# A new order of loads and work for attention and a feed-forward pair on one core

## The chip, the cores and the metric

The kernel runs on one core of a Trainium2 chip. The metric is device time in microseconds of one execution. The core has five engines with their own instruction queues: TensorE (PE, matmuls), VectorE (DVE), ScalarE (ACT), GpSimd (POOL) and SyncE (SP). Each runs its queue in order and waits at semaphores for the others. DMAs are issued by SP and by POOL.

## The reference

Four sequences of 768 positions and 8 heads of 64 are attended with a window, and the result goes through a feed-forward pair without a nonlinearity but relu and square:

```python
scores = scale * np.matmul(q, k.transpose(0, 1, 3, 2))      # q, k, v: (4, 8, 768, 64)
keep = is_global | is_local       # key < 8, or 0 <= query - key < 96
bias = -slopes[:, None, None] * dist[None, :, :]
a = softmax(np.where(keep, scores + bias, -1e9))
x = np.matmul(a, v).transpose(0, 2, 1, 3).reshape(3072, 512)
r = np.maximum(x @ w_in, 0.0)     # w_in: (512, 2048)
out = (r * r) @ w_out             # w_out: (2048, 512)
```

Inputs and output are float32; the kernel computes in bfloat16 with float32 sums.

## The kernel before

**Tiles.** The 3072 rows are cut into 24 tiles of 128 (0 to 23), six to a sequence; two tiles make one of 12 blocks. Tiles 0, 6, 12 and 18 are the first of their sequences. Because the window is shorter than a tile, a tile needs the keys and values of itself and of the tile before, whose first 8 columns are overwritten with the global keys (`gk`) and first 8 rows with the global values (`gv`).

**Attention of a tile j.** `ld` or `load` brings q, k and v, cast to bfloat16, through POOL's DMA queue (tile 0's q and k come over SP in float32). Up to tile 7 PE transposes q and k (`tr.0.j`, `tr.1.j`, L506) and ACT or DVE copies them out (`T.0.j`, `T.1.j`, L429/L433); from tile 8 on an SP DMA transposes them (`T.j`, L537). `sc.j.0` (L599) makes the scores: 16 matmuls into four banks, 8 into two for a first tile; `bias` (L579) precedes for tiles 0 to 2. `exp.j` (ACT, L665) empties a bank each. From tile 3 on `mul.j` (DVE, L690) multiplies with the masks `E`, or `E0` for a first tile, which `E0.0` and `E0.1` make (L439, L440). `pv` (L748) multiplies with v, `norm` (L778, L779) divides, and `trx` with `xT` (PE and a copy; from tile 8 on an SP DMA) transposes the result. `gate.j` (L480) is a tiny DVE write that lets POOL's load of tile j go.

**Feed-forward.** Blocks 0 and 1 take the first weight in the plain form: `s1.b.s` (L1061), `relu` (L865/L867), `sq` (L1098/L1100). All others, and the second weight from block 1 on, use seven products in place of eight: sums and differences of x (`xs`), of the weights (`isum`, `wsum`) and of hidden values (`sum`), then products `h.b.g.p1` to `p7` (L950) and `s2.b.p1` to `p7` (L1212). Between h products, ACT or DVE copies a bank out (`u`, L429/L433), DVE adds and applies relu (`c`, L995) and ACT or DVE squares (`q`, L1015/L1017). Block 0's second stage is plain (L1339). `part` and `o` (L1287) take the results out, `st` stores them. `wsum` and `isum` need all of a half's weights (`ld.win.s`, `ld.wout.s`).

**Order.** No scheduler runs on the chip or in the build: the text `ORDER` is a list of some 1,220 words, written out, and `Plan.run` emits each named operation at its place. `exp.3.0.1` is a name, `@A`, `@V`, `@P` choose ACT, DVE or POOL, and digits behind a colon are the PSUM banks, of which there are eight. Each engine's queue is its words of this list in order; nothing else fixes when an operation runs but what it waits for. POOL's loads run ahead of their place in the list as far as their buffers are free; `gv.j@P` copies stand in the same POOL queue. SP's queue holds `T.j`, `xT.j` and `st`.

At the start eight matmuls on zeros run (L372), and the list's `warm` adds eight more behind `tr.0.0` (L529 to L534). `COPY` names five tiles (14, 15, 19, 20, 22) whose keys are copied whole into `kl` (L703 to L719), so that the next tile's scores needn't wait for `gk`, which may only overwrite keys once the own tile's scores are made. `JOIN` could name stretches of scores that are made together with the preceding one (L615 to L630); it is empty. Four float32 buffers `u` are used in turn (L897). In the last block the product p3 is made in two parts of 192 and 64 columns, and each part's output operation waits for its own (L1261).

Of the kernel before, what the change touches and what calls it, by code (L numbers as in the profile page):

```python
# [63 lines left out]
tr.0.4:7 ld.q.5 ld.v.4 norm.2.1 mul.3.1 relu.0.6@A s1.0.3#2 gv.2@P pv.3.0:3 norm.3.0 trx.2:5 T.0.4@A pv.3.1:6
ld.win.1.0 norm.3.1 ld.win.0.1 xT.2@A sc.4.0:1047 exp.4.1.1 exp.4.1.0 tr.1.5:3 T.1.5@A s1.0.2:5 trx.3:6 xT.3@V
ld.win.0.0 ld.win.5.0 s1.0.2#2 s1.0.2#3 s1.0.2#4 relu.0.3@V exp.4.0.1 ld.v.5 gv.3@P exp.4.0.0 gk.4@V sq.0.6@V
relu.0.2@A s1.1.3:7 ld.win.7.0 relu.1.3@A load.6 s1.1.6:0 mul.4.1 tr.0.5:6 mul.4.0 sq.0.3@V s1.1.2:3 T.0.5@A ld.wout.3
pv.4.0:2 ld.wout.1 sq.0.2@V sc.5.0:4157 ld.wout.0 s1.0.4:6 relu.1.2@A exp.5.1.1 s1.0.1:3 sq.1.3@A exp.5.0.0 relu.0.4@V
s1.1.4:7 ld.wout.2 norm.4.0 pv.4.1:4 gv.4@P norm.4.1 sq.0.4@A load.7 exp.5.1.0 sq.1.2@A relu.1.4@A s1.0.0:6 gate.9
ld.wout.4 mul.5.0 s1.0.0#2 sq.1.4@A s1.0.0#3 s1.1.5:2 trx.4:1 exp.5.0.1 relu.1.6@V s1.1.1:4 ld.wout.5 s1.0.1#2  # L70
relu.1.1@A E0.1 mul.5.1 relu.1.5@A pv.5.0:7 s1.1.7:0 s1.1.0:5 sq.1.1@V norm.5.0 ld.wout.6 E0.0 sq.1.5@V tr.1.6:4
sq.1.6@A pv.5.1:2 relu.1.7@A tr.0.6:7 s1.0.0#4 norm.5.1 xT.4@A sq.1.7@A h.2.0.p2:0 ld.wout.7 T.1.6@V h.2.1.p2:1
trx.5:2 xT.5@V relu.1.0@A sq.1.0@A gate.14 h.2.0.p1:5 xs.2.0 s1.0.5:4 sum.1.2 s1.0.7:2 relu.0.1@A xs.2.1 gate.10
sum.1.0 sum.1.1 relu.0.0@A T.0.6@A sc.6.0:36 wsum.0.0 sum.1.3 sq.0.0@A sq.0.1@A s2.0.0.0:7 relu.0.7@A s2.0.1.0 load.9
exp.6.0.0 xs.2.2 s2.0.2.0 exp.6.1.0 s2.0.3.0 s2.0.0.1:2 s2.0.1.1 wsum.2.0 relu.0.5@A sq.0.7@A s2.0.2.1 load.8 mul.6.0
wsum.1.0 s2.0.3.1 tr.0.7:3 tr.1.7:6 gate.15 isum.0.0 h.2.1.p1:4 T.0.7@A s2.0.4.0 isum.0.1 s2.1.p1.0:3 isum.3.1 T.1.7@A
sq.0.5@A pv.6.0:6 isum.1.1 s2.0.4.1 s2.0.5.1 u.2.0.1@A c.2.0.c11 s2.0.5.0 gate.11 u.2.1.1@A h.2.1.p6 q.2.0.c11@A
isum.1.0 T.8 s2.0.6.1 u.2.1.2@A s2.0.6.0 isum.3.0 pv.6.1:0 h.2.0.p6 wsum.2.1 wsum.0.1 s2.1.p1.1 s2.0.7.1 c.2.1.c11
norm.6.0 gate.13 o.0.1@V st.0.1 s2.0.7.0 h.2.1.p7 part.1.p1@A s2.1.p6.0 u.2.0.2@A o.0.0@A u.2.1.3@A h.2.0.p7 h.2.1.p4
T.9 norm.6.1 wsum.3.0 u.2.0.3@A sc.7.0:1762 c.2.1.c21@A wsum.1.1 h.2.1.p5:0 c.2.1.c22 q.2.1.c11@A s2.1.p2.0:4  # L80
exp.7.1.0 exp.7.0.0 isum.2.1 load.10 h.2.0.p4 exp.7.0.1 mul.7.0 exp.7.1.1 s2.1.p2.1 isum.2.0 s2.2.p1.0:7 q.2.1.c21@A
mul.7.1 h.2.0.p5:1 s2.1.p6.1 part.1.p6@A trx.6:6 gate.12 c.2.0.c21@A load.12 pv.7.0:2 xT.6@A c.2.0.c22 q.2.1.c22@A
q.2.0.c22@A s2.2.p1.1 h.2.1.p3 s2.1.p7.0 wsum.3.1 o.1.p2 norm.7.0 h.2.0.p3 pv.7.1:5 s2.1.p7.1 q.2.0.c21@A st.0.0
c.2.1.c12 s2.1.p5.0 s2.1.p5.1 part.1.p7@A q.2.1.c12@A s2.1.p4.0 T.10 s2.1.p4.1 c.2.0.c12 gk.7@V q.2.0.c12@A o.1.p5
o.1.p4@A sc.8.0:6201 st.1.1 part.2.p1@A s2.1.p3.0 norm.7.1 sum.2.0 sum.2.1 s2.1.p3.1 trx.7:5 xT.7@V o.1.p3 h.3.0.p1:3
exp.8.1.0 gk.8@V h.3.1.p1:2 exp.8.0.0 exp.8.1.1 exp.8.0.1 h.3.0.p2:6 xs.3.0 u.3.1.1@A sc.9.0:1540 s2.2.p6.0 mul.8.0
xs.3.1 mul.8.1 u.3.0.1@A h.3.0.p6 exp.9.0.1 exp.9.1.1 gv.7@V h.3.1.p2:4 c.3.0.c11 h.3.1.p6 c.3.1.c11 exp.9.0.0
pv.8.0:0 s2.2.p6.1 pv.8.1:6 load.11 norm.8.0 u.3.1.2@A s2.2.p2.0:1 sum.2.2 gv.8@P q.3.1.c11@A norm.8.1 xT.8 h.3.1.p7
h.3.0.p5:4 u.3.0.2@A h.3.0.p7 s2.2.p2.1 exp.9.1.0 st.1.0 part.2.p6@A xs.3.2 u.3.1.3@A q.3.0.c11@A h.3.1.p5:0 s2.2.p7.0
u.3.0.3@A mul.9.1 mul.9.0 s2.2.p7.1 c.3.1.c22 T.12 c.3.0.c22 pv.9.0:6 h.3.1.p3 o.2.p2 h.3.0.p4 c.3.1.c12 load.15  # L90
norm.9.0 q.3.1.c22@A h.3.0.p3 s2.3.p1.0:5 s2.3.p1.1 c.3.0.c12 q.3.0.c22@A pv.9.1:0 c.3.0.c21@A part.2.p7@A norm.9.1
q.3.1.c12@A h.3.1.p4 q.3.0.c12@A h.4.0.p1:3 c.3.1.c21@A s2.2.p5.0 part.3.p1@A gk.9@V sc.10.0:6402 s2.2.p5.1
q.3.0.c21@A sum.3.0 sum.3.1 s2.2.p4.0 s2.2.p4.1 exp.10.1.0 sum.2.3 exp.10.0.0 exp.10.0.1 h.4.0.p2:4 T.11 u.4.0.1@A
exp.10.1.1 gk.10@V gv.9@A s2.3.p6.0 o.2.p5 mul.10.0 c.4.0.c11 xT.9 h.4.1.p1:6 o.2.p4@A mul.10.1 s2.2.p3.0 s2.2.p3.1
q.3.1.c21@A s2.3.p2.0:0 sum.3.2 u.4.1.1@A pv.10.0:2 pv.10.1:4 s2.3.p6.1 xs.4.0 gate.17 o.2.p3 part.3.p6@A xs.4.1
s2.3.p2.1 norm.10.0 h.4.0.p6 h.4.1.p6 q.4.0.c11@A gv.10@A norm.10.1 u.4.0.2@A load.13 s2.3.p7.0 sc.11.0:7124 u.4.1.2@A
sum.3.3 h.4.0.p7 h.4.1.p7 xs.4.2 exp.11.1.0 o.3.p2 exp.11.0.0 u.4.0.3@V s2.3.p7.1 sc.12.0:17 exp.11.1.1 exp.11.0.1
gate.16 xT.10 h.4.0.p4 c.4.0.c21@A mul.11.0 st.2.0 mul.11.1 h.4.1.p2:4 c.4.1.c11 exp.12.1.0 s2.3.p5.0 pv.11.0:2
pv.11.1:3 s2.3.p5.1 norm.11.0 part.3.p7@A h.4.0.p5:7 q.4.1.c11@A u.4.1.3@A norm.11.1 h.4.1.p5:4 q.4.0.c21@A gate.20
s2.3.p4.0 c.4.0.c22 load.14 s2.3.p4.1 h.4.0.p3 T.13 gate.18 load.16 c.4.1.c22 exp.12.0.0 h.4.1.p4 q.4.1.c22@A h.4.1.p3  # L100
xT.11 s2.4.p2.0:2 h.5.0.p1:3 q.4.0.c22@A o.3.p5 mul.12.0 c.4.0.c12 o.3.p4@A c.4.1.c21@A u.5.0.1@A c.4.1.c12 T.15
s2.3.p3.0 q.4.0.c12@A s2.3.p3.1 q.4.1.c12@V q.4.1.c21@A h.5.0.p2:1 o.3.p3 sc.13.0:5764 st.3.1 st.2.1 h.5.1.p1:0
exp.13.0.0 T.14 s2.4.p2.1 c.5.0.c11 exp.13.1.0 pv.12.1:1 q.5.0.c11@A s2.4.p1.0:5 xs.5.0 sum.4.0 pv.12.0:7 xs.5.1
s2.4.p1.1 mul.13.0 h.5.0.p6 gk.13@V u.5.1.1@A exp.13.0.1 h.5.1.p6 exp.13.1.1 h.5.0.p5:6 sum.4.1 norm.12.0 norm.12.1
h.5.1.p2:4 xs.5.2 mul.13.1 c.5.1.c11 h.5.1.p5:7 u.5.1.2@A sum.4.2 gate.19 part.4.p1@A h.5.1.p7 u.5.0.2@A h.5.0.p7
o.4.p2 u.5.0.3@A c.5.0.c22 pv.13.0:1 u.5.1.3@A norm.13.0 s2.4.p6.0 s2.4.p6.1 xT.12 st.3.0 q.5.1.c11@A T.16 part.4.p6@A
h.5.0.p4 pv.13.1:4 s2.4.p5.0 sum.4.3 c.5.0.c21@A h.5.0.p3 h.5.1.p4 q.5.0.c22@A s2.4.p7.0 norm.13.1 s2.4.p7.1 s2.4.p5.1
c.5.0.c12 q.5.0.c21@A kl.15@V part.4.p7@A c.5.1.c22 q.5.0.c12@A sc.14.0:1346 o.4.p5 s2.4.p4.0 xT.13 exp.14.0.1 kl.14@V
h.5.1.p3 gv.13@P q.5.1.c22@V c.5.1.c12 c.5.1.c21@A s2.4.p4.1 load.17 h.6.0.p1:4 s2.4.p3.0 s2.4.p3.1 exp.14.1.1
exp.14.1.0 exp.14.0.0 sc.15.0:0673 mul.14.1 mul.14.0 xs.6.0 o.4.p4@A xs.6.1 h.6.0.p2:1 o.4.p3 q.5.1.c12@A s2.5.p1.0:5  # L110
u.6.0.1@A c.6.0.c11 exp.15.0.0 exp.15.1.0 exp.15.1.1 sum.5.0 s2.5.p1.1 h.6.0.p6 u.6.0.2@A exp.15.0.1 sum.5.1 load.18
h.6.0.p5:2 part.5.p1@A pv.14.0:0 norm.14.0 pv.14.1:6 h.6.1.p1:1 u.6.1.1@A h.6.0.p7 gv.14@P st.4.0 s2.5.p6.0 u.6.0.3@A
# [1319 lines left out]
```

## Time and profile before

| what | before |
|---|---|
| time, median of 3 (lowest to highest) | 199.46 us (199.31 to 200.05) |
| time of the profiled execution | 199.37 us |
| its span | 197.6 us |
| PE busy | 191.9 us, 97% of the span |
| PE weight loads | 169.6 us, 86% |
| DVE busy | 173.2 us, 88% |
| ACT busy | 163.0 us, 82% |
| POOL busy | 80.4 us, 41% |
| DMA | 26.91 MB, mean 136 GB/s |

The span runs from the first to the last instruction. A matmul's end in the profile is modelled, and matmuls overlap, so PE's busy share says only that it had something in flight. Times in rows are microseconds from the span's start.

### The profile page before, as it was taken

What the parts mean: (1) busy time and instruction counts of PE and PEld (TensorE: products, weight loads), DVE (VectorE), ACT (ScalarE), POOL (GpSimd) and SP (SyncE); (2) the same over time, 40 slices, a digit from 0 to 9 for tenths busy, and PEclk for the clock granted to TensorE, in tenths of its full rate; (3) what the DMA queues carried; (4) which work ended last, traced back from release to release, by engine and by line L of the source; (5) the groups of instructions that cost most, each with busy time, mean ns of one, the idle gap of its engine ahead of it and who ended that gap; (6) DMA issues with size and microseconds to landing.
All of it is one profiled execution on the core that took longest, in us unless ns stands there. A gap on an engine that the chain in (4) does not pass through costs nothing.

```text
span 197.6 us, 6777 instructions
## 1 busy us (share of the span) xinstructions
PE 191.9 (97%) x2776; PEld 169.6 (86%) x2776; DVE 173.2 (88%) x423; ACT 163.0 (82%) x335; POOL 80.4 (41%) x101
## 2 busy tenths in 40 slices
...
GB/s 127 153 158 171 181 181 185 182 202 159 139 209 191 75 200 88 145 174 210 151 129 203 114 124 194 160 121 92 136 81 116 154 55 56 27 30 163 0 106 106
DMA packets 111857, 26.91 MB, mean 136 GB/s; under 512 B 103379, under 2 KB 109011, under 8 KB 111827
## 3 DMA queue, kind: packets, MB, share of 16 engines
...
HBM read 27.26 MB, written 6.29 MB: 170 GB/s over the span
## 4 chain that ended last, share of the span: by engine, by line
PE 95%; DVE 2%; issue 1%; ACT 0%; DVEq 0%
PE bank L1212 35%; PE bank L950 32%; PE bank L1061 7%; PE bank L599 6%; PE bank L748 5%; PE bank L1339 4%; PE bank L372 2%; PE bank L506 2%; PE bank L532 1%; DVE qkT L433 1%; PE bank L816 1%; PE bank L579 0%; ACT qkT L429 0%; DVE o L1287 0%; DVE v L433 0%
## 5 line engine op out<-in xcount | busy, mean ns | idle before, releaser
L1015 ACT ACTIVATE hs<-hr 128x512 bf16<-128x512 f32 x72 | 44.8, 641 | 5.1 <-DVE hr L995 4.7
L665 ACT ACTIVATE esc<-bank 128x512 bf16<-128x512 f32 x78 | 42.9, 614 | 1.3 <-PE bank L599 1.0
L1212 PE MATMUL bank<-wsum,hsum 128*128 128x256 bf16 x264 | 36.2, 273 | 0.0
L1212 PEld LDWEIGHTS <-hsum 128*128 128x128 bf16 x360 | 32.1, 98 | 4.1 <-issue 0.5
L995 DVE CUSTOM_DVE_ANT_0 hr<-bank,early 128x512 f32<-128x512 f32 x45 | 30.4, 685 | 2.5 <-PE bank L950 1.5
L950 PEld LDWEIGHTS <-win 128*128 128x128 bf16 x480 | 29.7, 98 | 1.0
L950 PEld LDWEIGHTS <-qk_first 128*128 128x128 bf16 x480 | 29.7, 98 | 1.0
L429 ACT COPY early<-bank 128x512 f32<-128x512 f32 x42 | 24.5, 591 | 3.6 <-PE bank L950 3.3
L690 DVE TENSOR_TENSOR at<-esc,E 128x1024 bf16<-128x1024 bf16 x39 | 26.7, 696 | 0.1
L1212 PEld LDWEIGHTS <-hs 128*128 128x128 bf16 x264 | 24.0, 98 | 2.6
L310 POOL DMA_DIRECT2D qk<-in_q_dram x18 | 16.0, 890 | 21.9 <-DMA qkT<-qk 20.6
L1212 PE MATMUL bank<-wout,hs 128*128 128x256 bf16 x176 | 24.9, 273 | 0.0
L310 POOL DMA_DIRECT2D v<-in_v_dram x18 | 16.0, 888 | 18.3 <-DVE v L480 14.9
L950 PE MATMUL bank<-xT,win 128*128 128x128 bf16 x320 | 23.4, 219 | 0.0
L431 POOL COPY v<-v 8x520 bf16<-8x520 bf16 x8 | 5.7, 718 | 43.3 <-PE bank L748 43.3
L950 PE MATMUL bank<-xs,qk_first 128*128 128x128 bf16 x320 | 22.8, 219 | 0.0
L779 DVE TENSOR_TENSOR x<-bank,rs 128x256 bf16<-128x256 f32 x48 | 20.4, 425 | 1.7
L865 ACT ACTIVATE hr<-bank 128x512 f32<-128x512 f32 x33 | 19.4, 598 | 1.3 <-PE bank L950 0.4
L748 PE MATMUL bank<-v,at 128*128 128x65 bf16 x352 | 17.8, 193 | 0.0
L1287 DVE TENSOR_TENSOR o<-bank,part 128x256 f32<-128x256 f32 (+2 forms) x34 | 13.8, 410 | 3.3 <-PE bank L1212 3.2
L429 ACT COPY part<-bank 128x256 f32<-128x256 f32 x29 | 10.9, 375 | 7.1 <-PE bank L1212 6.9
L310 POOL DMA_DIRECT2D qk<-in_k_dram x18 | 16.1, 897 | 0.9 <-DMA win<-in_moe_w_in_dram 0.5
...
## 6 DMA issues: line engine op xcount, KB each, us to landing
...
```

The lines of the kernel that those rows point to most:

```text
L310: nc.gpsimd.dma_start(out=dst, in_=src)
L429: nc.scalar.copy(dst, src)
L665: nc.scalar.activation(out=tiles[tag, j, g][:, odd], in_=tiles.pop(("sc", j, odd, g)).rearrange("p a c -> p (a c)"), func=Act.Exp, scale=s ...
L690: nc.vector.tensor_mul(at, tiles.pop(("esc", j, g)), bias)
L748: nc.tensor.matmul(out=po[:, hi, :], lhsT=tiles["at", j, g][:, odd, at * P : (at + 1) * P], rhs=v_sb[kj][:, h, :], start=(i == 0), stop=(i ...
L779: nc.vector.tensor_tensor(out=x[:, 4 * hf : 4 * hf + 4, :], in0=po[:, :, :D], in1=rs.to_broadcast([P, 4, D]), op=Alu.mult,)
L865: nc.scalar.activation(dst, src, Act.Relu)
L950: nc.tensor.matmul(out=tiles["h", blk, g, bank][:, n], lhsT=left_[:, s, k], rhs=right_[:, k], start=opens and n == 0 and k == 0, stop=k == ...
L995: nc.vector._custom_dve(TENSOR_ADD_SAT, out=hr, in0=src, in1=tiles.pop(("u", blk, g, i)), s0=float("inf"), s1=0.0,)
L1015: nc.scalar.activation(hs, hr, Act.Square)
L1061: nc.tensor.matmul(out=hT[:, c, cols], lhsT=w_in_sb[s][:, kt, c * P : (c + 1) * P], rhs=tiles["xT", blk][:, kt, cols], start=(kt == 0), st ...
L1212: nc.tensor.matmul(out=tiles["acc", blk, bank][:, cols], lhsT=left_[:, s], rhs=right_[:, cols], start=first and s == 0, stop=s == NSTEP - ...
```

## The change

The list is written anew. In it:

- POOL's first load is k of tile 1; before it was a piece of the first weight. v of tile 0, q, k and v of tiles 1 to 3, q and k of tile 4 and q of tile 5 come ahead of the first weight piece (`win.1.0`, fourteenth), and k of tile 5 after the third.
- The first products with the first weight (`s1`) come behind `pv.3.1`; before they came behind `pv.2.1`, ahead of the scores of tile 4.
- `warm` is gone, and with it its eight matmuls.
- `E0.1` and `E0.0` come with tiles 0 and 1; before they came with tile 5.
- The scores of tiles 7, 13 and 19 are made in one stretch with those of 6, 12 and 18, into six banks at once (`sc.6.0:273561`, `sc.12.0:507463`, `sc.18.0:205371`).
- Attention of the later tiles stands earlier against the blocks: scores of tile 23 before `s2.8.p6.0`, before the change behind `s2.9.p1.1`.
- The letters differ: q 67 on ACT and 13 on DVE (72 and 8 before), u 53 and 7 (57 and 3), c 17 and 3 (20 and 0, of those that may go to either), relu 11 and 5 (13 and 3), sq 10 and 6 (11 and 5), part 25 and 8 (29 and 4), `gv` 2 on ACT, 10 on POOL (4 and 8), 4 on DVE in both.

Beside the list: `COPY` is empty, so five tiles take `gk` instead of `kl`. A tile's `pv` also waits for the preceding tile's v. The `u` buffers are handed out as they come free instead of in turn. In the last block both output operations of p3 wait for its last product.

```diff
 ORDER = """
-tr.0.0:0 warm:7 tr.1.0:1 T.1.0@V bias.0.0:23 T.0.0@A sc.0.0 ld.win.3.0 exp.0.0.0 ld.k.1 tr.1.1:4 bias.1.0:5670 T.1.1@V ld.q.1
-tr.0.1:1 ld.v.0 exp.0.1.0 T.0.1@V sc.1.0 exp.1.0.1 pv.0.0:2 ld.q.2 tr.0.2:3 norm.0.0 ld.k.2 T.0.2@V ld.k.3 exp.1.1.1
...
-T.1.4@V xT.1@V pv.2.1:0 ld.k.5 ld.win.2.0 exp.3.1.1 gk.3@A ld.win.2.1 norm.2.0 s1.0.3:2 mul.3.0 s1.0.6:4 ld.win.4.0
...
+ld.k.1 tr.0.0:0 tr.1.0:1 bias.0.0:23 T.1.0@A tr.1.1:4 T.0.0@V ones.6 ld.q.1 sc.0.0 exp.0.1.0 tr.0.1:5 T.0.1@V
+exp.0.0.0 bias.1.0:6701 E0.1 ld.v.0 pv.0.0:3 T.1.1@A pv.0.1:5 sc.1.0 exp.1.1.1 ld.q.2 norm.0.0 norm.0.1 exp.1.0.1
+tr.0.2:2 T.0.2@V ld.k.2 tr.1.2:4 T.1.2@V ld.q.3 gk.1@V ld.v.1 trx.0:3 bias.2.0:5120 E0.0 tr.0.3:4 ld.k.3 sc.2.0
+exp.1.0.0 pv.1.1:6 T.0.3@V xT.0@A exp.1.1.0 pv.1.0:3 gv.1@V exp.2.1.0 tr.1.3:4 T.1.3@V exp.2.0.0 ld.v.2 pv.2.0:7
+exp.2.0.1 gk.2@V sc.3.0:1542 exp.2.1.1 pv.2.1:0 norm.1.0 ld.q.5 exp.3.0.0 tr.0.5:3 ld.k.4 gate.9 norm.1.1 trx.1:6
+exp.3.1.0 ld.q.4 exp.3.1.1 gk.3@V exp.3.0.1 tr.1.4:1 tr.0.4:5 norm.2.0 norm.2.1 trx.2:7 ld.v.3 ld.win.1.0 ld.win.3.0
+ld.win.0.0 ld.k.5 T.0.4@A T.1.4@A mul.3.0 gv.2@P pv.3.0:2 mul.3.1 ld.win.0.1 sc.4.0:0451 xT.1@A norm.3.0 exp.4.0.0
+T.0.5@V pv.3.1:6 gv.3@V s1.0.1:2 s1.0.1#2 norm.3.1 xT.2@A trx.3:3 s1.0.3:0 s1.0.3#2 relu.0.1@A xT.3@A s1.0.0:7
+s1.1.3:6 tr.1.5:2 exp.4.0.1 exp.4.1.1 ld.win.2.0 relu.1.3@A T.1.5@A gk.4@A s1.1.1:3 s1.0.0#2 relu.0.3@V s1.0.0#3
...
+sc.6.0:273561 wsum.2.0 exp.6.0.0 load.8 s2.0.4.0 s2.0.5.0 s2.1.p1.0:2 s2.1.p1.1 wsum.0.1 wsum.1.1 T.8 exp.6.1.0
...
+s2.1.p5.0 s2.1.p5.1 gate.14 wsum.2.1 sc.8.0:1740 exp.8.1.0 gate.11 load.11 exp.8.0.0 h.3.0.p2:5 exp.8.0.1 s2.1.p7.0
...
-    JOIN = set()
-    COPY = [14, 15, 19, 20, 22]
+    JOIN = {(7,0),(13,0),(19,0)}
+    COPY = []
...
-        if j == 0:
-            def emit_warm(e):
-                for _ in range(NKEEP):
-                    nc.tensor.matmul(out=psum(), lhsT=zero[:, :P], rhs=zero, start=True, stop=True)
-
-            plan.op(("warm",), {"PE": 0.216 * NKEEP}, emit_warm, key=base)
...
-        def open_sc(gs, j=j):
-            for n, (g, odd) in enumerate((g, odd) for g in gs for odd in range(2)):
+        def open_sc(gs, at=0, j=j):
+            for n, (g, odd) in enumerate(((g, odd) for g in gs for odd in range(2)), at):
                 tiles["sc", j, odd, g] = psum(n).rearrange("p (a c) -> p a c", a=4)
...
                 for f, gs in gs:
-                    f(e, gs)
+                    f(e, gs, at)
+                    at += 2 * len(gs)
                 return
...
-                deps.append(glob.get(("v", j - 1)))
+                deps += [glob.get(("v", j - 1)), land["v", j - 1]]
...
-    u_next = [0]
+    u_free = list(u_ring)
...
-                for o, cols in zip(done, cuts):
+                for o, cols in zip([done[-1]] * len(cuts), cuts):
```

More of the change, by code (lines that the diff above doesn't have):

```diff
@@ L63 @@
-T.1.4@V xT.1@V pv.2.1:0 ld.k.5 ld.win.2.0 exp.3.1.1 gk.3@A ld.win.2.1 norm.2.0 s1.0.3:2 mul.3.0 s1.0.6:4 ld.win.4.0
[L64 to L112, printed above, removed]
```

159 lines of the change are left out of this document (100 added, 59 removed).

## The prediction

> **What bounds the kernel now.** First the page, for the engines; then the chain of work that ended last, for where TensorE (PE) waits; then the windows view, for what VectorE (DVE) has left; then groups and timeline, for prices.
>
> ```profile
> span 197.6 us, 6777 instructions
> PE 191.9 (97%) x2776; PEld 169.6 (86%) x2776; DVE 173.2 (88%) x423; ACT 163.0 (82%) x335; POOL 80.4 (41%) x101
> ```
>
> ```profile
> 1.19 3.60 PE bank L372 x8
> 5.64 2.41 PE bank L532 x8
> 8.05 0.45 PE bank L506 x4
> 8.53 0.70 DVE qkT L433
> 11.62 0.62 PE bank L599 x16
> 14.47 0.62 PE bank L599 x16
> 18.29 1.32 PE bank L1061 x16
> 21.11 0.55 PE bank L599 x16
> 25.10 0.87 PE bank L1061 x8
> 26.22 0.55 PE bank L599 x16
> 38.99 3.56 PE bank L1339 x16
> 45.73 0.45 PE bank L950 x8
> 47.61 0.44 PE bank L1212 x4
> ```
>
> The chain (start, length) is a latency chain up to about 18 us: transpose, copy, scores of tile 1 (11.62), of tile 2 (14.47). Scores of tile 4 follow at 21.11, of tile 5 at 26.22. From there PE is never idle:
>
> ```profile
> core 0: us, PE busy (x) PEld busy (x) DVE busy (x) ACT busy (x) POOL busy (x), PEclk, DMA share, GB/s
> 26.15:183.50 157.35, 157.35 (x2355) 141.84 (x2353) 147.59 (x343) 137.75 (x282) 55.45 (x66) 1.00 1.25 138
> 38.60:53.00 14.40, 14.40 (x158) 10.08 (x158) 14.12 (x30) 11.01 (x23) 7.88 (x9) 1.00 1.92 170
> 136.90:159.70 22.80, 22.80 (x358) 21.16 (x356) 21.64 (x49) 20.87 (x43) 2.63 (x3) 1.00 0.74 118
> ```
>
> The first window runs from the scores of tile 5 to the first second-stage product of the last block. PE is busy for all 157.35 us. "Busy" may hide small waits, so I set it against the list: its PE operations between these two names, at their back-to-back spacing (0.45 for an h product, 0.44 for an s2 product, 0.87 for a whole s1, by the chain's rows), are 154.9 us. So at most 2.5 us in 157 is not product work: the kernel is PE-bound behind its head. DVE has 9.8 us idle in this window, ACT 19.6. The fullest DVE stretches that cost PE nothing are the other two rows: 14.12/14.40 = 98.1% and 21.64/22.80 = 94.9%.
>
> The profiled execution is 199.37 us (197.6 of span and 1.8 around it), 0.1 under the median 199.46. The sum starts from 199.4.
>
> **The change part by part.** Prices:
>
> ```profile
> L779 DVE TENSOR_TENSOR x<-bank,rs 128x256 bf16<-128x256 f32 x48 | 20.4, 425 | 1.7
> L1017 DVE TENSOR_TENSOR hs<-hr 128x512 bf16<-128x512 f32 x8 | 5.5, 686 | 0.1
> L433 DVE COPY early<-bank 128x512 f32<-128x512 f32 x3 | 2.1, 692 | 1.7 <-ACT esc L665 1.6
> L433 DVE COPY part<-bank 128x256 f32<-128x256 f32 x4 | 1.6, 412 | 0.0
> L433 DVE COPY kl<-qkT 128x512 bf16<-128x512 bf16 x3 | 1.2, 394 | 0.0
> L439 DVE COPY E<-E 128x512 bf16<-128x512 bf16 x2 | 0.9, 462 | 0.0
> 24.09 1.29 DVE L690 TENSOR_TENSOR at<-esc,E 128x1024 bf16<-128x1024 bf16 x2
> ```
>
> ```profile
> 1.25 0.56 SPq L319 DMA_DIRECT2D plain<-in_k_dram  x1
> 1.34 0.89 POOL L307 DMA_DIRECT2D win<-in_moe_w_in_dram  x1 [0.17 <-issue]
> 2.22 0.90 POOL L307 DMA_DIRECT2D qk_first<-in_k_dram  x1
> 17.31 2.12 ACT L665 ACTIVATE esc<-bank 128x512 bf16<-128x512 f32 x4
> 21.04 0.23 PE L599 MATMUL bank<-qkT 64*128 64x128 bf16 x2
> 21.45 0.22 PE L599 MATMUL bank<-qkT,qkT 64*128 64x128 bf16 x2
> 194.16 0.36 DVE L1287 TENSOR_TENSOR o<-bank,part 128x192 f32<-128x192 f32 x1 [0.84 <-PE bank L1212]
> 194.57 0.28 PE L1212 MATMUL bank<-wout,hsum 128*128 128x64 bf16 x4 [0.45 <-DVE o L1287]
> 194.88 0.22 DVE L1287 TENSOR_TENSOR o<-bank,part 128x64 f32<-128x64 f32 x1 [0.37 <-PE bank L1212]
> ```
>
> *Head, until the scores of tile 5.* POOL's first issue is now k of tile 1, not a weight piece, so every load of tiles 1 to 3 is issued 0.9 us earlier (1.34 for 2.22). Tile 0's k comes over SP and landed 6.0 us after its issue at 1.25 (page, longest landing of `plain`, below); it was used only at 8.05, behind the eight fill-in matmuls of L532, which are gone. Its new landing lies between 1.25+3.1 and 1.25+6.0; I take 6.4, since no weight piece shares the DMA engines with it. From there, with matmuls at half speed until about 10 (below): transposes to 7.2, biases to 8.1, k of tile 1 to 8.5, scores of tile 0 to 9.0, two exps at 0.50 (four take 2.12) to 10.2, copy of k of tile 1 on ACT to 10.7, scores of tile 1 at 10.9: 0.7 earlier than 11.62.
>
> Before, the next step, to the scores of tile 2, took 2.85. I work out 2.9 for it and 2.4 for the one after, with the same exps, since both `E0` operations (a copy of 0.46 and a maximum after it, each) now stand between DVE's norms and copies of these tiles instead of behind tile 4: scores of tile 3 at 16.2. Scores of tile 4 stand behind tile 3's four exps and two `T` copies on ACT, six at 0.50: 20.0, against 21.1, so attention gains one microsecond. But the list has no s1 product ahead of this point, where before the first starts at 18.29 and fills PE. The first now comes behind the second product of tile 3, at 20.9; then `trx.3` waits for `norm.3.1` on DVE (L779's 0.43, with a reciprocal and the copy `gv.3` ahead of it; I take 1 us, to 22.3), and six s1 products (0.87 each) and two transposes follow. Scores of tile 5 at 27.2, against 26.2: **+1.0 us** (from -0.6, if k lands at 5.5 and the half speed ends at 7, to +1.8).
>
> The weights, now behind thirteen loads, are hardly late themselves: the fourteenth issue is at 1.34+13x0.88 = 12.8, and with the 5.6 to 8.7 us of the landing row below it is there at 18.4 to 21.5; the work at 20.9 covers all but the end of that, 0.6. `gv.2` on POOL now stands ahead of `win.0.1`: POOL waits for tile 2's second product (about 17) and issues the rest of the weights 1.4 us later; `win.0.1` is needed at about 25.5, so 4 us of cover.
>
> ```profile
> POOL v L431 <- PE bank L748: 43.3, 5, 23.0
> DMA to landing us min/median/max: 3.1/4.6/6.0
> ...
> DMA to landing us min/median/max: 5.6/6.4/8.7
> ...
> DMA to landing us min/median/max: 3.4/5.0/8.2
> ...
> DMA to landing us min/median/max: 3.1/3.8/7.4
> ```
>
> (POOL's waits before `gv`; then landing times of `plain`, of the issues at L307, of those at L310, and of `qkT`'s transposes.)
>
> *PE's list behind tile 5.* The same products. A stretch of scores ends with a pause: 16 matmuls take 0.55 in the chain, though they start 0.41/14 apart (21.04 to 21.45), 0.44 to 0.47 in all. Three joined stretches save three pauses of about 0.1, -0.3; 0.2 us of work that stood ahead of tile 5 now stands behind. **-0.1.** Six banks held at once leave two: at each join PE has 0.7 to 2.2 us of listed products that need none of the six before the first exp (0.50) gives one back, so nothing; without that cover 0.5 each.
>
> *`COPY` emptied.* Five whole `kl` copies (0.39 and a small one) become 32-column copies. Scores of tile j+1 now wait for a copy that waits for scores of tile j; at least 1.8 us of products lie between. Nothing on the path.
>
> *Tail.* Both parts of the last output wait for the last product; PE's wait of 0.45 goes. The last add ended at 195.1 behind add, matmuls, add; now matmuls, add, add: 0.2 less, but the two stores follow each other on SP. **-0.1.**
>
> *Letters, the term that decides.* Between the same two names the new list gives DVE 9 squares, 4 u copies, 2 relus and 3 first parts more that ACT had: 18 at 0.60 (two that follow each other take 1.29, so one costs 1.29-0.69) = 10.8. Further 3 adding parts and one mul come in by order (2.4), two `part` copies and one `T` (1.0); both `E0`, three `kl`, a `gv`, small copies and a gate go (-3.1). Net +11.1 us: 147.6+11.1 = 158.7 us of DVE in a stretch where PE's list needs 157.35+1.2 = 158.6 (its own operations there are 156.1 for 154.9). DVE would have to be busy without a break for 158 us while it waits for PE and ACT in turn. Price: 0 if it is; at 98.1% the stretch takes 161.8, +3.2; at 94.9% 167.2, +8.6. I also count the rises of DVE's listed work over PE's: the largest before, carried without a pause, is 3.25 us; the new list has seven larger ones (4.2, 3.9, 3.75, 3.5, 3.4, 3.4, 3.3), 2.6 us over it together. That lies near the 98.1% row; I take **+2.6**.
>
> Sum: 199.4 + 1.0 - 0.1 - 0.1 + 2.6 = **202.8 us**. Within 0.5% (1 us) a measurement of this kernel can hardly be told from no change.
>
> **The clock.** L372's eight 512-column matmuls start 0.43 to 0.45 apart, L1339's sixteen 0.22, and L532's eight take 2.41, some at each speed: half speed until about 7 us, though PEclk reads 1.00 throughout. The fill-in matmuls kept PE busy until then; without them I took 10, three microseconds later. [...]
>
> **Rivals.**
> 1. *DVE is not waited for.* What it does late (sums, weight differences, squares) is needed late. For it: 14 us at 98.1% cost nothing. Against: ten times that length. 199.4+1.0-0.2 = 200.2: no change. It decides if DVE's idle time in the stretch falls under 1 us with PE full.
> 2. *The head wins* (faster). k of tile 0 lands by 5.5, full speed from 7, scores of tile 1 by 9.9 and of tile 5 by 25.4 (-0.8), DVE waited for nowhere: 198.3. For it: the 0.9 us of POOL's first issue and the fill-in matmuls. Against: PE stands without s1 between 18.3 and 20.9. It decides when tile 5's scores start before 25.9.
> 3. *Transposes come late.* Attention runs ahead: tile 12's scores stand behind 66 us of listed PE work for 71.5. `gate.11` stands behind the scores of tile 8 (27.2 and 30 us of listed work: 57.5), so k of tile 11, third in POOL's queue, issues near 60, lands 5.0 or 8.2 later, is transposed in 3.8 or 7.4: 69 or 76, needed at 71 (27.2+43.6). With one such miss of about 3 us: 205.8.
> [...]
>
> **How the numbers follow.** Forecast (200.8 to 205.5) 0.50; rival 1 0.17, rival 2 0.13, rival 3 0.10, rival 4 0.10. Slower by over 0.5%: 0.70; within: 0.17; faster: 0.13. The range 198.8 to 206.0 leaves out most of rival 2 and the worst of DVE's upper price; the forecast's own is above.
>
> **What would show it.** Right: scores of tile 5 at 27; DVE above 97% from there to the last block; PE's listed work short of its time there by 4 to 6 us instead of 2.5, with waits of matmuls for DVE (`qkT`, `hr`, `hsum`, `at`) in the table; ACT's share down by some 5 points. [...]

## The result, and the profile after

| | before | after |
|---|---|---|
| median (lowest to highest), 4 runs each | 199.41 us (199.31 to 200.05) | 205.16 us (203.57 to 206.19) |
| ratio, with its 95% interval | 1 | 1.0274 (1.0201 to 1.0347) |
| profiled execution | 199.37 us | 205.58 us |
| its span | 197.6 us | 203.8 us |

The change makes the kernel slower by 5.75 us. Here and below, medians and ratios leave out executions that took over 1.5% longer than the fastest of the same kernel. The profiled execution is 6.2 us longer than that of before, and the following accounts for these 6.2. Its page:

```profile
span 203.8 us, 6768 instructions
...
PE 192.5 (94%) x2764; PEld 169.6 (83%) x2768; DVE 180.6 (89%) x434; ACT 153.3 (75%) x317; POOL 81.3 (40%) x103
...
PE   7988999999999679999979999999999999999993
...
PEclk9999999999999969999999999999999999999999
```

PE's busy time is about the same (191.9 before), its share falls from 97% to 94%. In the slices of 5.1 us, PE drops to 6 and 7 behind 66 us and to 7 behind 102 us, and the granted clock drops once, behind 71 us. The table of waits of PE (wait, then total us, times, longest) names what it stood for:

```profile
PE bank L593 <- DMA qkT<-qk: 2.5, 1, 2.5
PE bank L593 <- DVE x L773: 1.9, 3, 0.9
PE bank L371 <- DVE early L360: 1.2, 1, 1.2
...
PE bank L742 <- DVE at L684: 0.3, 1, 0.3
```

The code lines have moved by a few: L593 are the scores, L530 the DMA transposes of q and k, L834 those of x, L773 the multiply of `norm`, L479 the gates, L944 and L1205 the products `h` and `s2`. The third row is the start, the same before. The first two are new. The windows view divides the span (stretch, length, PE, PE's weight loads, DVE, ACT, POOL busy, granted clock, DMA share, GB/s):

```profile
24.46:191.40 166.94, 161.82 (x2370) 145.11 (x2373) 153.87 (x348) 130.87 (x271) 57.69 (x71) 0.99 1.19 130
24.00:60.00 36.00, 35.59 (x472) 28.92 (x474) 34.20 (x78) 31.33 (x64) 21.80 (x28) 1.00 1.71 186
60.00:80.00 20.00, 16.81 (x249) 14.90 (x246) 15.05 (x42) 15.04 (x31) 7.47 (x10) 0.91 1.44 124
80.00:112.00 32.00, 30.60 (x500) 28.15 (x498) 28.81 (x72) 28.19 (x60) 15.70 (x19) 1.00 1.78 159
112.00:185.00 73.00, 72.88 (x1087) 67.50 (x1086) 69.86 (x150) 52.68 (x112) 13.19 (x17) 1.00 0.69 97
```

The first row is the stretch from the scores of tile 5 to the first second-stage product of the last block. PE lacks 5.1 us in it, 3.2 of them between 60 and 80 us and 1.4 between 80 and 112. Behind that PE is full (72.88 of 73.00) with DVE at 69.86, or 95.7%. Before, from 60 to 80 us:

```profile
60.00:80.00 20.00, 20.00 (x316) 18.61 (x315) 18.89 (x47) 18.20 (x38) 9.81 (x12) 1.00 1.46 137
```

A busy share misses small waits and half speed. So I took each PE operation's time to the next one's start and subtracted its back-to-back spacing; what is left is time without product work, in us (what half speed costs is in it):

| stretch | before | after |
|---|---|---|
| 0 to 26 (in before the 1.72 of the fill-in matmuls count as lost) | 8.3 | 7.0 |
| 26 to 60 | 1.1 | 1.5 |
| 60 to 80 | 0.6 | 5.6 |
| 80 to 112 | 1.5 | 3.2 |
| 112 to the last matmul | 2.5 | 2.2 |
| last matmul's start to the span's end | 2.9 | 3.6 |

Together 6.2 more (16.9 and 23.1), which is the difference of the spans. Two places carry it. In the timeline (start, length, in brackets the idle time before and its releaser) the first is this:

```profile
68.82 0.60 PE L1205 MATMUL bank<-wsum,hsum 128*128 128x256 bf16 x4
71.90 0.23 PE L593 MATMUL bank<-qkT 64*128 64x128 bf16 x2 [2.48 <-DMA qkT<-qk]
...
73.06 0.26 PE L593 MATMUL bank<-qkT 64*128 64x128 bf16 x1 [0.70 <-DVE x L773]
...
74.40 1.91 PE L1205 MATMUL bank<-wsum,hsum 128*128 128x256 bf16 x8
```

PE wants the scores of tile 11 at 69.2; `T.11`, the transposes of its q and k, lands at 71.85. Then the scores' second half waits for a bank that `norm.10` empties, and DVE is late with that. From 73.1 on PE runs at half speed: eight `s2` matmuls take 1.91 that took 1.04 at 60.35. Half speed lasts to 76.45; the windows view of these microseconds has the granted clock at 0.62:

```profile
72.50:77.00 4.50, 3.94 (x40) 3.22 (x40) 3.40 (x10) 2.96 (x6) 0.26 (x1) 0.62 0.60 123
```

So one late transpose cost 2.65 + 0.9 of waiting and, at half speed for 3.4 us, some 1.4 more. The two gaps ahead of the slow stretch, 2.65 and 0.9, have nine matmuls between them; why half speed follows them, and why for 3.4 us, the trace doesn't show.

Why `T.11` is late stands in POOL's and SP's rows of the timeline:

```profile
56.34 0.87 POOL L309 DMA_DIRECT2D v<-in_v_dram  x1 [7.82 <-DVE v L479]
...
58.06 0.90 POOL L309 DMA_DIRECT2D qk<-in_k_dram  x1
...
63.26 0.94 POOL L309 DMA_DIRECT2D qk<-in_k_dram  x1
```

```profile
62.91 1.24 SPq L530 DMA_TRANSPOSE qkT<-qk  x1
64.26 1.63 SPq L834 DMA_TRANSPOSE xT<-x  x1
...
68.89 4.67 SPq L530 DMA_TRANSPOSE qkT<-qk  x2
```

POOL stands 7.82 us at `gate.11`, which the list has behind the scores of tile 8. Then the nine loads of tiles 11, 13 and 12 go out back to back; `gate.13` and `gate.12` stand far ahead, in block 0's part of the list, and hold nothing back by then. k of tile 11 lands about 62.9. SP issues its transpose at once, into the loads of the other two tiles. The landing times of the transposes, first those issued from 50 to 56 us, then from 62 to 75:

```profile
L530 SPq DMA_TRANSPOSE qkT<-qk x3: 1267/1287/1337, 51.1 to 53.9; - x3
...
DMA to landing us min/median/max: 3.1/3.2/3.6
...
L530 SPq DMA_TRANSPOSE qkT<-qk x3: 1236/1238/2782, 62.9 to 72.3; - x3
...
DMA to landing us min/median/max: 3.1/5.3/8.9
```

3.1 to 3.6 us when POOL issues nothing, 8.9 for `T.11`. `xT.8` behind it took 8.2, and its landing frees the x buffer that `norm.10` needs: DVE's 3.56 us of waiting, the second part of PE's stall. The other way round as well: the loads issued at 62.39 and 63.26 landed 5.9 and 9.0 us later. In this trace both kinds came late beside each other (8.9 and 9.0 us), and a transpose took up to 2.9 times the 3.1 us of the shortest without loads.

The second place is the chain of work that ended last (start, length):

```profile
97.39 5.26 DMA xT<-x
...
102.74 0.06 DVE xs L916
...
103.84 0.43 DVE x L773
...
104.32 0.60 PE bank L593 x15
```

`xT.13` stands on SP behind `T.15` and `T.16`, is issued at 97.39 and lands 5.26 us later. `xs.6.0` needs it and holds DVE's queue; `norm.14` behind it comes late, and the scores of tile 16 wait for its bank: 1.0 + 0.5. POOL issued five loads from 98.71 to 102.18, beside this transpose; that they made it late was not isolated.

Together 2.65 + 0.9 + 1.4 + 1.0 + 0.5 = 6.5 of the 8.8 us without work between 60 and 112 us, where before has 2.1. In this execution the head wins 1.3 of it back, and the end loses 0.7.

### The profile page after: what moved, and what is told of

The parts are those of the page before. It is cut to its first block, busy times and chain, and to the rows that moved or that the text cites. A ratio compares the mean times of both kernels' runs of the same rounds, so it can differ in the third digit from the quotient of the medians.

```text
span 203.8 us, 6768 instructions
## 1 busy us (share of the span) xinstructions
PE 192.5 (94%) x2764; PEld 169.6 (83%) x2768; DVE 180.6 (89%) x434; ACT 153.3 (75%) x317; POOL 81.3 (40%) x103
## 4 chain that ended last, share of the span: by engine, by line
PE 45%; DVE 3%; DMA 3%; issue 0%; DVEq 0%
PE bank L1205 23%; PE bank L944 18%; DMA xT<-x 3%; PE bank L742 2%; PE bank L593 2%; DVE hr L989 1%; DVE o L1280 1%; DVE hsum L1160 1%; DVE x L773 0%; DVE at L684 0%; DVE part L432 0%; DVE rs L772 0%; DVE xs L916 0%; DVEq L1420 0%; DVEq L989 0%
## 5 line engine op out<-in xcount | busy, mean ns | idle before, releaser
L1008 ACT ACTIVATE hs<-hr 128x512 bf16<-128x512 f32 x67 | 41.3, 638 | 6.6 <-DVE hr L989 4.8
L1205 PE MATMUL bank<-wsum,hsum 128*128 128x256 bf16 x264 | 37.1, 277 | 0.0
L1205 PEld LDWEIGHTS <-hsum 128*128 128x128 bf16 x360 | 33.0, 99 | 4.1 <-DVE hsum L1160 0.2
L989 DVE CUSTOM_DVE_ANT_0 hr<-bank,early 128x512 f32<-128x512 f32 x47 | 32.0, 686 | 1.7 <-PE bank L944 1.2
L944 PEld LDWEIGHTS <-qk_first 128*128 128x128 bf16 x480 | 30.0, 98 | 2.8 <-issue 0.8
L944 PEld LDWEIGHTS <-win 128*128 128x128 bf16 x480 | 30.2, 98 | 1.0 <-issue 0.2
L684 DVE TENSOR_TENSOR at<-esc,E 128x1024 bf16<-128x1024 bf16 x39 | 26.9, 690 | 0.3 <-ACT esc L659 0.2
L1205 PEld LDWEIGHTS <-hs 128*128 128x128 bf16 x264 | 24.1, 98 | 2.8
L773 DVE TENSOR_TENSOR x<-bank,rs 128x256 bf16<-128x256 f32 x48 | 20.4, 424 | 5.2 <-DMA xT<-x 3.6
L430 POOL COPY v<-v 8x520 bf16<-8x520 bf16 x10 | 6.8, 678 | 44.7 <-PE bank L742 44.7
L1205 PE MATMUL bank<-wout,hs 128*128 128x256 bf16 x176 | 24.6, 272 | 0.0
L944 PE MATMUL bank<-xT,win 128*128 128x128 bf16 x320 | 24.1, 219 | 0.0
L944 PE MATMUL bank<-xs,qk_first 128*128 128x128 bf16 x320 | 23.6, 219 | 0.2 <-DVE xs L916 0.2
L859 ACT ACTIVATE hr<-bank 128x512 f32<-128x512 f32 x28 | 16.8, 605 | 4.2 <-PE bank L1054 2.9
L593 PE MATMUL bank<-qkT 64*128 64x128 bf16 x192 | 13.2, 219 | 4.9 <-DMA qkT<-qk 2.5
L593 PEld LDWEIGHTS <-qkT 64*128 64x128 bf16 x352 | 10.2, 95 | 9.0 <-issue 4.5
L742 PEld LDWEIGHTS <-at 128*128 128x128 bf16 x352 | 14.9, 98 | 2.8 <-ACT at L659 0.7
```

What stands on the lines that cost most here:

```text
L593: nc.tensor.matmul(out=tiles["sc", j, odd, g][:, at, :], lhsT=left[j - 1][half, pair, :] if kt else qkT[j % NKT][half, 1, pair, :], rhs=qk ...
L684: nc.vector.tensor_mul(at, tiles.pop(("esc", j, g)), bias)
L742: nc.tensor.matmul(out=po[:, hi, :], lhsT=tiles["at", j, g][:, odd, at * P : (at + 1) * P], rhs=v_sb[kj][:, h, :], start=(i == 0), stop=(i ...
L773: nc.vector.tensor_tensor(out=x[:, 4 * hf : 4 * hf + 4, :], in0=po[:, :, :D], in1=rs.to_broadcast([P, 4, D]), op=Alu.mult,)
L859: nc.scalar.activation(dst, src, Act.Relu)
L944: nc.tensor.matmul(out=tiles["h", blk, g, bank][:, n], lhsT=left_[:, s, k], rhs=right_[:, k], start=opens and n == 0 and k == 0, stop=k == ...
```

## Experiments

The diffs show words of the list around each edit, against the changed kernel's list where nothing else is said; ratios are to the kernel before, with their 95% interval. The change itself stands at 1.0274 (1.0201 to 1.0347).

**What stalls the transposes: moving the gates.** Theory: the loads beside `T.11` make it slow. Rival: its buffers or DVE's letters do. First only the gates were moved.

```diff
-sq.0.2@V pv.5.1:3 gate.13 norm.5.0
+sq.0.2@V pv.5.1:3 norm.5.0
...
-gv.9@A sum.2.2 norm.9.0
+gv.9@A sum.2.2 gate.13 norm.9.0
```

> The changed kernel with one word moved: gate.13 stands behind sum.2.2 (about 64.7 us) and no longer in block 0, so that POOL's loads of tiles 13 and 12 are issued from about 65 us on and not at 58.7 to 63. Theory T (transposes): T.11, issued at 62.67, then has no load beside it and lands by 66 instead of 71.6; the waits of TensorE for scores of tile 11 (2.65 and 0.89 us) and the half-speed stretch behind them go: 199.5 to 202 us, the clock at 1.00 between 72 and 77, a small new wait (up to 1 us) possible at tile 12's scores. Theory D (VectorE's letters cost the time): 205 us as the changed kernel, within 1 us.

Measured: 1.022 (1.0158 to 1.0281). This doesn't test the theory: `load.13` stood in the list ahead of the moved gate, so POOL's load was not held by it. The gate's write came behind the load and overwrote one column of tile 13's v.

```diff
-sq.0.2@V pv.5.1:3 gate.13 norm.5.0
+sq.0.2@V pv.5.1:3 norm.5.0
...
-pv.7.1:7 norm.7.1 s2.1.p2.1
+pv.7.1:7 norm.7.1 gate.11 s2.1.p2.1
...
-sc.8.0:1740 exp.8.1.0 gate.11 load.11
+sc.8.0:1740 exp.8.1.0 load.11
...
-h.3.0.p6 c.3.0.c11 exp.9.0.1
+h.3.0.p6 c.3.0.c11 gate.13 exp.9.0.1
```

> The changed kernel with two words moved: gate.11 stands behind norm.7.1 (load of tile 11 about 2.3 us earlier) and gate.13 behind c.3.0.c11 (about 62 us). Theory T: T.11 is issued near 60 and lands by 64, T.13 and T.12 by 74, all before TensorE's list needs them: 199 to 201.5 us, a little under the run with gate.13 alone. Theory D: 205 us, within 1 us.

Measured: 1.0228 (1.0171 to 1.0284), with the same flaw in `gate.13`. So in effect `gate.11` alone was moved, to `norm.7.1`, and that gains nothing that these intervals show.

```diff
-sq.0.2@V pv.5.1:3 gate.13 norm.5.0
+sq.0.2@V pv.5.1:3 norm.5.0
...
-u.3.0.1@A exp.9.1.1 load.13 u.3.1.1@A
+u.3.0.1@A exp.9.1.1 u.3.1.1@A
...
-gv.9@A sum.2.2 norm.9.0
+gv.9@A sum.2.2 gate.13 load.13 norm.9.0
```

> The changed kernel with gate.13 and load.13 moved together behind sum.2.2 (about 64.7 us), so that POOL's loads of tiles 13 and 12 are now really held back (from 58.7 to about 65 us) while T.11 is in flight. Theory T: T.11 lands by 66 and not at 71.6, the waits of 2.65 and 0.89 us and the half-speed stretch go; T.12 may come up to 2 us late at tile 12's scores: 200 to 202.5 us. Theory D (VectorE's load as such costs the time): 204 to 206 us.

Measured: 1.0473 (1.0448 to 1.0497), slower than the change itself. Its timeline:

```profile
62.83 1.23 SPq L530 DMA_TRANSPOSE qkT<-qk  x1
65.30 0.88 POOL L309 DMA_DIRECT2D v<-in_v_dram  x1 [6.03 <-DVE rs L772]
...
69.67 0.23 PE L593 MATMUL bank<-qkT 64*128 64x128 bf16 x2
...
73.08 4.72 SPq L530 DMA_TRANSPOSE qkT<-qk  x2
...
81.90 0.71 PE L593 MATMUL bank<-qkT 64*128 64x128 bf16 x10 [5.49 <-DMA qkT<-qk]
```

With the loads of tiles 13 and 12 held back until 65.30 `T.11`, issued at 62.83 as before (62.91), lands at 67.6 and not at 71.85, and the scores of tile 11 wait no more. But now `T.13` and `T.12` land at 78 and 81.9, PE waits 5.49 us for the latter, and 4.9 us at half speed follow (81.9 to 86.8, granted clock 0.50). The first half supports the theory, with every load in place; the second shows that the chain from gate to load to transpose to scores has no slack for three tiles: a gate moves the wait, it doesn't take it away.

Two more places for the loads of 11 and 13, the second with tile 17's gate moved too:

```diff
+pv.7.1:7 norm.7.1 gate.11
...
+sum.1.3 load.10 load.11 T.10
...
+h.3.0.p6 c.3.0.c11 gate.13 load.13
```

In the second also:

```diff
-s2.2.p5.1 o.2.p5 gate.17 norm.11.0
+s2.2.p5.1 o.2.p5 norm.11.0
...
+c.4.0.c21@A norm.13.1 gate.17
```

> The changed kernel with gate.11 behind norm.7.1 and gate.13 with load.13 behind c.3.0.c11: load of tile 11 issued from about 54 us, of tiles 13 and 12 from about 62. Theory T: T.11 issued near 60 and landed by 64, T.13 and T.12 by 75: no wait of a microsecond left between 60 and 80, 199.5 to 201 us, with the wait at 102 us (1.5 us) still there. Theory D: 204 to 206 us.

> As the run before it, and gate.17 behind norm.13.1 (about 94.5 us in the changed kernel's time), so that loads of tiles 17 to 19 are issued some 4 us later and T.15, T.16 and xT.13 have fewer loads beside them. Theory T: xT.13, which took 5.26 us and held VectorE until 102.7, lands earlier, and the waits of 1.04 and 0.52 us behind it go: 1 to 2 us under the run before it, 198 to 200 us. Rival: the loads only meet the next transposes (xT.14, T.17) and gv.14 is late for the second product of tile 15: no gain, 200 to 202 us.

Measured: 1.0359 (1.0308 to 1.041) and 1.0299 (1.0266 to 1.0333), no better than the change; the second's six executions spread from 205.48 to 211.21 us. By the code q of tile 11 can't be loaded before `T.8` has emptied one of three buffers (`NQ`), so an earlier gate lets go only v. That is argued for these two, not isolated. Whether moving the gate of tile 17 gains something of the second stall these runs don't settle.

**The loads taken away.** The decisive one: the change without the nine loads of tiles 11 to 13.

```diff
             def emit_load(e, j=j):
+                if j in (11, 12, 13):
+                    return
                 load_v(j)
...
```

> The changed kernel without POOL's loads of q, k and v of tiles 11, 12 and 13 (nine DMAs of 128 KB left out; these tiles are computed from what lies in their buffers, so the output is not the reference's). T.11 to T.13 then wait for no load, and no load lies beside the transposes between 56 and 68 us. Theory T: the waits of TensorE for transposed q and k and the half-speed stretch behind them vanish, about 5 us less, 199 to 201 us, with the wait near 102 us still there. Theory D (the letters, VectorE or ScalarE late): the wait turns up on VectorE or ScalarE instead, 203 us or more.

Measured: 1.0132 (1.0082 to 1.0181), 202.13 us, 3.0 less than the change. From 60 to 80 us and from 80 to 112 the windows view gives, and the transposes issued from 56 to 90 us land in:

```profile
60.00:80.00 20.00, 20.00 (x346) 18.38 (x344) 19.37 (x51) 19.71 (x42) 7.71 (x9) 1.00 0.71 96
80.00:112.00 32.00, 30.30 (x484) 27.89 (x482) 28.57 (x70) 27.70 (x59) 11.73 (x15) 1.00 1.59 160
```

```profile
DMA to landing us min/median/max: 3.1/3.4/5.9
```

PE is full from 60 to 80, the clock stays at 1.00, and `T.11` to `T.13` land within 3.1 to 3.4 us (the row's median is 3.4). The order of PE, DVE and ACT is the change's, letters and all. So the first stall comes from the loads, and not from the letters. Taking the loads away also takes their own lateness away, so this run can't say what part their traffic has; the run with `load.13` held back (67.6 for 71.85) and the next one show that. The second stall stays, and its loads are still there:

```profile
PE bank L595 <- DVE x L775: 1.5, 2, 1.2
```

**One buffer more.** If the chain of loads is at fault, a fourth buffer for q and for k should let each load go earlier, with nothing left out.

```diff
-    NQ, NKT, NV = 3, 2 * TPB, 10
+    NQ, NKT, NV = 4, 2 * TPB, 10
...
+mul.6.0 sum.1.2 gate.11
...
+sum.1.3 load.10 load.11 T.10
...
+h.3.0.p1:6 norm.8.0 gate.13 load.13
...
+c.4.0.c21@A norm.13.1 gate.17
```

> The changed kernel with four buffers for loaded q and k instead of three, so that load of tile 11 needn't wait for T.8; gate.11 behind sum.1.2 (load of tile 11 from about 49 us instead of 56), gate.13 with load.13 behind norm.8.0 (about 59.5), gate.17 behind norm.13.1. Theory T: T.11 lands by 62, T.13 and T.12 by 74 at the latest, no wait over 1 us at 69 to 76: 199 to 201 us. Rival: loads of tile 11 beside T.8 to T.10 make the scores of tiles 8 and 9 late instead (1 to 3 us), or T.12 still comes behind 76: 202 to 207 us.

Measured: 1.0159 (1.0106 to 1.0213), 202.80 us; the interval just touches that of the change.

```profile
60.00:80.00 20.00, 20.00 (x344) 18.18 (x339) 19.33 (x52) 19.71 (x43) 11.22 (x13) 1.00 1.50 162
80.00:112.00 32.00, 31.37 (x503) 29.01 (x501) 30.89 (x74) 28.78 (x61) 14.18 (x17) 1.00 1.74 163
```

The first stall is gone with all loads in place, and the second is down to small waits. The loads of tile 11 now go out from 51.19 to 53.81, beside `T.8` to `T.10`, and these three transposes land after 5.2 to 6.3 us, where they took 3.1 to 3.6 in the changed kernel: the traffic of the loads by itself stretched them. The scores of tile 8 wait 0.6 us for that, which is the rival of the expectation, if smaller. The profiled span is 200.3, 2.7 over before; by the same accounting some 2.1 of it lie in waits of 0.8 and less between 36 and 112 us. What the others are due to isn't settled. In this execution k of tile 0 came late, too, which bears on the head (below).

**The letters.** Theory of the prediction: DVE carries 11 us too much. Then 19 operations moved from DVE to ACT in the changed kernel should win, and 19 moved the other way in the kernel before should lose.

```diff
-relu.1.0@V
+relu.1.0@A
...
-part.3.p6@V
+part.3.p6@A
...
-q.6.1.c22@V
+q.6.1.c22@A
...
```

and in the list before:

```diff
-relu.1.1@A
+relu.1.1@V
...
-q.2.1.c12@A
+q.2.1.c12@V
...
-u.3.0.1@A
+u.3.0.1@V
...
```

> The changed kernel with 19 operations between the scores of tile 5 and the last block given back from VectorE to ScalarE (5 q, 4 u, 3 c, 2 relu, 1 sq, 4 part), so that VectorE has some 10.5 us less to do there, as in the kernel before. Theory D: 202.6 us or less (2.6 us less than 205.2). Theory T: the waits at 69 and 102 us are for transposes and stay: 204.2 to 206.2 us.

> The kernel before with 19 operations between the scores of tile 5 and the last block given from ScalarE to VectorE (5 q, 4 u, 3 c, 2 relu, 1 sq, 4 part), some 10.5 us more for VectorE: 158 us in a stretch of 157.35. Theory D: 199.4 + 2.6 = 202 us (up to 208). Theory T: VectorE late by a little delays nothing: 199.4 to 200.4 us.

Measured: 1.0511 (1.0461 to 1.056) and 1.0529 (1.0465 to 1.0593). Both are slower than the kernel they were made from, and by amounts that neither theory had. Waits of PE, first of the one, then of the other:

```profile
PE bank L593 <- DVE x L773: 2.8, 3, 2.0
...
PE bank L944 <- ACT early L428: 1.2, 1, 1.2
PE bank L1205 <- ACT part L428: 0.9, 1, 0.9
```

```profile
PE bank L599 <- DVE hr L867: 1.5, 1, 1.5
PE bank L950 <- DVE u L433: 1.2, 1, 1.2
...
PE bank L1212 <- DVE part L433: 1.2, 2, 0.9
```

In each, PE waits for copies of the engine that got more (in the first `early` and `part` on ACT, in the second `hr`, `u` and `part` on DVE). The first's largest row, 2.8, is the two stalls of the changed kernel again, at tiles 11 and 16. Each also has 3.4 us at half speed behind its waits, from 73.9 to 77.3 and from 42.1 to 45.5 us (granted clock 0.91 from 60 to 80 us in the first, 0.95 from 24 to 60 in the second). In the second, DVE has 154.69 us of work in the 166 between 27 and 193 us and isn't full:

```profile
27.00:193.00 166.00, 158.06 (x2290) 138.62 (x2290) 154.69 (x357) 127.16 (x260) 54.72 (x65) 0.99 1.18 128
```

93%, and yet PE loses 8 us there. So a full engine isn't needed for the loss. The waits fit that a copy PE needs now stands behind something else in that engine's queue: a list is written for its letters, and 19 changed ones break it in either direction. That is argued from the rows; no run moved one copy alone. These runs say nothing about what the letters would cost in a list made for them; the changed kernel is such a list, and there PE is full at 95.7%.

**The fill-in matmuls.**

```diff
-tr.0.0:0 warm:7 tr.1.0:1
+tr.0.0:0 tr.1.0:1
```

> The kernel before without its word warm: the eight fill-in matmuls behind the first transpose are left out, and nothing else. Theory H (the head's gain came from leaving them out): tile 0's second transposes start near 5.2 instead of 7.9 and tile 5's scores up to 1.7 us earlier: 197.7 to 198.7 us. Theory O (the gain came from the order of loads, and in the old order k of tile 1 or the first weight pieces set the pace): 199 to 199.8 us. Theory C (the fill-in matmuls keep the clock): half speed beyond 7 us, 200 us or more.

Measured: 1.001 (0.9987 to 1.0033), no difference. The scores of tile 5 come at 24.93 with 1.72 us of matmuls fewer, and PE waits 1.13, 0.35 and 0.42 for k of tiles 1, 2 and 3 instead. What tile 5 gained hardly reaches the end of the kernel.

**Parts of the new list on the old.** The first 36 us (without the gates of tiles 9, 12 and 13) and the first 56 us of the changed list, continued with before's order; the code around the list is the changed kernel's. Against the list before:

```diff
-tr.0.0:0 warm:7 tr.1.0:1 T.1.0@V
+ld.k.1 tr.0.0:0 tr.1.0:1 bias.0.0:23
...
```

and in the second, further on, up to the same `s2.1.p5.1` as in the changed list:

```diff
-    JOIN = set()
+    JOIN = {(7,0)}
```

> The changed kernel's list up to the last s1 product of the second block (about 36 us), and from there the operations that are left in the order, with the letters, of the kernel before (its five whole key copies, no joined stretches, banks renamed to fit). Theory H (the new head is worth 1.3 to 1.6 us, and all of it and more was lost behind it): tile 6's scores come 1 to 1.6 us earlier than before and nothing behind loses them: 197.6 to 198.6 us, faster than both kernels. Rival: the old order behind meets its loads and transposes at other times and waits there, or the seam costs the gain: 199.4 us or more.

> As the run with the new head on the old order, but the seam lies at about 56 us (behind s2.1.p5.1, ahead of the scores of tile 8; the joined scores of tiles 6 and 7 stay), where all pieces of the second weight have landed (the last at 45.7 in the changed kernel): the first part is the changed kernel's list, the rest is the old order with its letters and its key copies. Theory W (the first seam lost its time because the second weight lands 1 to 4 us later in the new order of loads, while tile 11's scores are wanted at 80 us and not at 69 in the old order): the changed kernel's lead of 0.6 to 0.9 us at this place is kept, no wait for the second weight, none of the waits of 2 us and more for T.11 or xT.13: 198 to 199.2 us. Rival S (any seam in a list written out for its own times costs more than that): 200 us or more.

Measured: 1.0247 (1.0208 to 1.0286), 204.60 us, and 1.0103 (1.0054 to 1.0152), 201.76 us. In the first, PE waits for the second weight, whose loads come later in the new order than before's block 0 wants them, and then runs at half speed until 45.8 (512-column matmuls of up to 631 ns, 379 in the median):

```profile
PE bank L1333 <- DMA wout<-in_moe_w_out_dram: 3.2, 3, 2.0
PE bank L945 <- DVE xs L917: 1.7, 1, 1.7
```

So it can't price the head. In the second that is gone, as is the wait for `T.11`, and what is left are waits of under 0.8 us at the seam (57.7, 59.4, 61.3). It is 3.4 us under the changed kernel, and bounds what the new first 56 us can cost at 2.1, with the seam's waits and the changed kernel's 0.7 at the end in it. None of these kernels beats the one before.

## Why the prediction was right and wrong

The sign was right, and the time (202.8, range to 206.0) was 2.4 short. The sum was made of the wrong terms: of its +3.6 for head and letters next to nothing was found, and the transposes, which it had at 0, cost 6.5. So sign and range came out by luck. What happened was rival 3, which had a chance of 0.10; that its 205.8 lies so near is luck as well, since it holds the same 3.6.

- *Head, predicted +1.0: not found; in this execution it is -1.7.* k of tile 0 was used at 5.2, not 6.4, and full speed came at 4.9, not 10. The first rows of PE in the timeline:

```profile
4.58 1.28 PE L505 MATMUL bank<-ident,plain 128*128 128x128 f32 x8
...
6.54 0.40 PE L593 MATMUL bank<-qkT 64*128 64x128 bf16 x8
```

  The scores of tile 0 start at 6.54 (predicted 9.0), of tile 3 at 13.36 (16.2), of tile 4 at 17.70 (20.0), of tile 5 at 24.48 (27.2; before 26.15). The steps between were about right: 4.3 us from tile 3's scores to tile 4's where I had 3.8, and 6.8 to tile 5's where I had 7.2. What failed was "I take 6.4", from the slow end of what the rows allowed, and "I took 10": no run shows that this follows from leaving out the fill-in matmuls (without them alone the ratio was 1.001), and half speed ended between 4.5 and 10.3 us in different profiles. Rival 2's sign, scores of tile 5 before 25.9, came true (its time is 198.4 by its own terms, not 198.3). But the profiled execution is on the lucky side: with the same head the other profiles have 24.7 to 26.9, the middle one 25.1. And the kernel before has no fixed 26.15: the run that moved letters to DVE has its head unchanged (every moved letter stands behind the scores of tile 5), and there they came at 25.21, with full speed from 4.55, where the profile before has half speed until 6.7:

```profile
25.21 0.23 PE L599 MATMUL bank<-qkT 64*128 64x128 bf16 x2
```

  So these profiles can't tell the two heads apart; the end of half speed at the start moves by more from profile to profile than the heads differ. In the run with four buffers k of tile 0 landed late and half speed lasted until 10.3, as the sum had it (10), and the scores of tile 5 came at 26.29; in no profile here did half speed at the start last longer:

```profile
6.39 1.12 PE L505 MATMUL bank<-ident,plain 128*128 128x128 f32 x4 [0.75 <-DMA plain<-in_k_dram]
8.15 0.63 PE L505 MATMUL bank<-ident,qk_first 128*128 128x128 bf16 x4
```

- *Letters, "the term that decides", predicted +2.6: wrong, some +0.3, at most +0.6.* Outside the two stalls the accounting has 0.4 more than before from 26 to 60 us, 0.2 more from 60 to 112 and 0.3 less behind. DVE's work in the stretch came to 153.87 us and not 158.7, 92.2% of it and not over 97%. By the trace's DVE instructions of that stretch, some 13.7 us came in (the prediction has 14.2) and some 7.0 went, where it counted 3.1. From 112 to 185 us, where no transfer was late, 95.7% cost PE 2.1 us in 73, against 1.9 before. The mistake was to price a share. A share close to a row that cost nothing was read as the beginning of a cost, although that row itself (98.1%) had none. ACT's share fell from 82% to 75%, where some 5 points were predicted.
- *PE's list and the joins, −0.1: not isolated.* The joined stretch of tiles 6 and 7 still has a pause of 0.41 in it (46.06 to 46.47); those of 12 and 13 and of 18 and 19 run through.
- *`COPY` emptied, 0: no sign against it.* PE's table has no wait for a copy of keys from tile 14 on.
- *Tail, −0.1: not as said.* The wait of 0.45 is gone (0.6 to 0.1 in the accounting), but the last matmul to the end takes 0.7 longer, since both adds follow it: +0.2.

```profile
200.46 0.49 DVE L1280 TENSOR_TENSOR o<-bank,part 128x192 f32<-128x192 f32 x2 [0.47 <-PE bank L1205]
```

- *Transposes, 0 in the sum: the step that failed most, +6.5.* Rival 3 had the place (tile 11), the gate (57.5 by its sum, 56.3 in the trace), the landing (69 or 76; 71.85) and the need (71; 69.2, since the head won), and a price of 3 us, for one miss. It missed two things: that the stall brought 3.4 us of half speed, and that the x transposes stand in the same SP queue and come late too, `xT.8` in the first stall and `xT.13` in the second, at 102.7. And its chance was low because I took 5.0 and 3.8 us, medians over the whole run, for a load and a transpose that run in a burst of nine loads. The rows had the 8.2 and 7.4 beside them, and its own text the landing at 76.

Two signs against the forecast were there: scores of tile 5 before 25.9, as rival 2 has them, and PE waiting for a DMA (2.5 us, for `qkT`). The loss of PE's time that was to show as waits for `hr`, `hsum` and `at` was hardly there (0.3 twice for `at`, 0.2 for `hr`).

Left open: what the 2.1 us of small waits with four buffers are due to; what the letters and the head are worth by themselves; what makes `xT.13` late; the joins were not undone.
